# Query projections written from PSUM as 128x256 pieces, and queries stacked through DRAM instead of directly

## Chip, cores and metric

The kernel runs on one core of a Trainium2 chip. The metric is device time in microseconds (us) of one execution; the kernel before took 758.66 us (median of three runs, 758.6 to 760.47 us).

## What is computed

One transformer block on `x` of 2048 tokens by 512 features, in float32:

```python
qkv = layernorm(x) @ wqkv                      # 32 heads of 16 for q, k and v
scores = q @ k.T * 16 ** -0.5                  # per head
mask = (i - j >= 0) & (i - j < 256)            # sliding window of 256 tokens
o = softmax(where(mask, scores, -1e9)) @ v
h = x + o @ wo
z = layernorm(h)
out = h + (sigmoid(z @ w_gate) * (z @ w_up)) @ w_down      # 1376 inner features
```

## The kernel before

The 2048 tokens are 16 tiles of 128 and eight batches `b` of 256. Matrix products are made from float16 numbers: each operand is split into a high and a low half, and `mm3` (L359-362) issues three matmuls for each product, high by high, high by low and low by high. Such a split is made by two operations on a PSUM tile: the high half is copied out by ScalarE or VectorE (`copy`, which records L315 for ScalarE and L317 for VectorE), then VectorE computes what is left as a `scalar_tensor_tensor`.

**Order of the work.** Every step of the kernel is a piece of a generator. `TABLE`, a list of names, says which piece takes its next step, and with `/a`, `/v` or `/g` on which engine (ScalarE, VectorE, GpSimd) where a step may run on several. `Order` (L232-288) does no planning on the chip: the rows on each engine stand in the order of the table, and each engine works through its own rows in order. All the transfers are issued by SyncE (SP), also in order. `RINGS` (L302) gives the number of buffers of each kind; `s`=3 and `mm`=2 are PSUM rings, `chunk`=3 is the ring of weight chunks and normalised rows.

**Start.** `wqkv`, `wo` and the tiles of x are loaded. The greatest absolute value of each weight matrix is found (`am`, partly by ScalarE at L327, partly by VectorE at L329), passed through PE (L340) and made into a scale (`fq`, L344-348 on VectorE), with which the weights are split (ScalarE L315 `W<-wq,sq`, VectorE L481). The tiles of x are normalised (VectorE L497-501, ScalarE L510), split, and transposed by PE (L534) into `xT` (copied out at L315 or L317).

**Queries and keys.** `do_qk(b, c, jj)` (L562-587) makes for a batch the half `jj` of the queries (c=0) or the keys (c=1): 24 matmuls of 128x256 into a PSUM tile of 128 x 2 x 256, then the split into a staging tile, `sq` for queries and `sk` for keys. A key tile is split as one piece of 128x512. A query tile is split in two pieces of 64x512, since the partitions 0-63 hold one head of a pair and 64-127 the other, and the two go to different blocks of `sq`; the other blocks of `sq` stay zero, written once at the start. 

**Stacks.** The score matmuls contract over 96 rows: a stack holds high, high and low halves of the queries (`SQ`) against high, low and high halves of the keys (`SK`), 32 rows each. `do_queries(b, p)` (L606-614) fills a quarter of `SQ` for a batch by three transfers from `sq`, 128 KB each: four quarters, so twelve transfers in each batch and 96 in all. The next batch but one may overwrite `sq` when the four quarters are copied. `do_keys(b)` (L589-604) first writes `sk` to DRAM (`mem<-sk`, two transfers) and then reads the stack back (`SK<-mem`, 384 KB, twice in each batch).

**Attention.** `do_s` (L636-661) computes scores 128 rows by 320 columns into the `s` ring, and VectorE takes each row's maximum with the mask (L647, `junk<-sp,mask`, followed by the read of its accumulator, `mq`): 512 such row maxima in all. `do_m` turns them into four further rows of the stacks, so that `do_st` (L681-725) gives transposed scores with the maximum taken off (contraction over 100 rows, L711-722). ScalarE takes the exponentials (L689, into `pa` and `pb`), GpSimd cuts the mask (L695, L700), and `do_pv` (L729-761) multiplies with the values. The value projection (`W1v`, three 128x512 matmuls at each step), the output projection and the second layer norm stand between these on all the engines, and so do the scaling and splitting of the weights of the second half (`W0u`, `W`, `Tg`), whose `chunk` loads run throughout.

**Second half.** Gate, up and down products follow (L1096 and around). The last attention steps and the first gate matmuls overlap at about 400 to 440 us.

The parts that the change and the prediction touch are `do_qk`, `do_queries`, `do_keys`, the table, and `stacked`, which arranges the columns of `wqkv` before the launch.

Of the kernel before, what the change touches and what calls it, by code (L numbers as in the profile page):

```python
# [35 lines left out]
P = 128  # L36
# [29 lines left out]
load_w0 load_x0 load_w3 load_x1 load_w1 load_w2 zeros0 load_x3 load_w4 load_x2 load_w14 load_w10 load_w9 load_w15 load_w11 ln0*2 prep0/a*2 ln1 prep0/a ln0/v  # L66
load_w8 load_w12 load_x4 load_w5 load_w13 load_w6 load_x6 load_w7 ln1 prep0/v ln0/a prep0 ln1/a ln0/g prep0*2 ln4 ln1/a ln0 ln1/g zeros1 fill0 fill1 ln0/v
warm2 prep1/a prep0/a prep0 prep0/a prep0 prep0/a ln1 warm1 prep0 prep0/a ln1/a ln4 prep0 ln2 prep2/a qk0 ln2 qk1 qk0 prep2/a qk0 warm3 qk0 ln3 prep2/a ln5
prep2/a ln3 ln3/a qk0 qk1 qk0*3 qk1 ln2/v prep2 qk0/a prep2 qk1*5 ln4/v ln2/v ln3/v ln5 ln2/g qk0 ln4/a qk1/a prep2 warm4 warm0 ln2 warm5 qk1 fill2 ln3/g
# [4 lines left out]
amax1/a amax2 qk2*6 v1 qk2/v v1 qk2 v1 keys0 qk7 keys0 qk7*2 v1 qk7 prep3/a prep3/v prep3/g prep3/v ln9 amax0/v fill2 ln6 fill0 fill2 fill0 qk7*2 v1/v qk7
qk6*2 qk7 amax3/a amax4 queries3 qk6 warm8 qk7/v qk6*3 qk7 prep3/v keys0 qk6*2 v3 qk6/v v3 qk6 v3 queries2 amax7 queries5 queries6 keys1 ln4 v3 ln4/v amax4/a
amax2/a ln5/a v3/a prep3/g ln5/g ln7 fill1 fill0 fill2 s0*3 s0.0 s0.1 s0.2 s0*2 v4 s0.3 s0.4 s0*2 s0.5 s0.6 queries4 queries5 keys1 queries7 keys0 amax8 amax6
s1 ln5 s1 s1.0 s2 s1.1 v4 prep3/a*2 ln6/a s2.0 ln10 s0 s1 v4 s1 v4 s0.7 s1.2 s1.3 s1*2 s1.4 s1 s1.5 s1 s1.6 ln6/a ln5/a ln6/g prep3/g ln10 v4/a ln7/a amax7/a
# [1662 lines left out]
```

## Time and profile before

| what | us |
|---|---|
| median of three runs | 758.66 |
| the profiled execution, its own time | 758.37 |
| its span on the core | 756.0 |
| PE busy with matmuls | 732.3 |
| VectorE busy | 622.5 |
| ScalarE busy | 447.5 |
| GpSimd busy | 336.3 |

The time of an execution is some 2.4 us longer than the span that the profiler shows on the core. PE is the engine of matmuls; its weight loads (PEld) run beside them. The profile's windows give the busy time of each engine in a stretch of the span, its groups give the mean time of a kind of instruction, and its chain follows the work that ended last backwards from the end.

### The profile page before, as it was taken

What the parts mean: (1) busy time and instruction counts of PE and PEld (TensorE: products, weight loads), DVE (VectorE), ACT (ScalarE), POOL (GpSimd) and SP (SyncE); (2) the same over time, 40 slices, a digit from 0 to 9 for tenths busy, and PEclk for the clock granted to TensorE, in tenths of its full rate; (3) what the DMA queues carried; (4) which work ended last, traced back from release to release, by engine and by line L of the source; (5) the groups of instructions that cost most, each with busy time, mean ns of one, the idle gap of its engine ahead of it and who ended that gap; (6) DMA issues with size and microseconds to landing.
All of it is one profiled execution on the core that took longest, in us unless ns stands there. A gap on an engine that the chain in (4) does not pass through costs nothing.

```text
span 756.0 us, 18726 instructions
## 1 busy us (share of the span) xinstructions
PE 732.3 (97%) x6930; PEld 486.6 (64%) x6930; DVE 622.5 (82%) x1863; ACT 447.5 (59%) x784; POOL 336.3 (44%) x431
## 2 busy tenths in 40 slices
PE   4999999999999999999999899999999999999997
PEld 3777777777787677787665544454544755757573
DVE  6979999989888878788888999976899779587562
ACT  6845988787787877687768976523332224231401
POOL 7563557534553556445656612342230315345611
PEclk9999999999999999999999999999999999999999
DMA  9894665745948645445536768541775745545533
GB/s 324 209 249 125 146 132 109 178 123 103 194 110 171 120 84 146 92 80 141 112 78 143 182 144 240 137 77 37 153 174 123 129 91 112 101 98 110 116 53 97
DMA packets 182394, 100.96 MB, mean 134 GB/s; under 512 B 153440, under 2 KB 159584, under 8 KB 182304
## 3 DMA queue, kind: packets, MB, share of 16 engines
q1 hardware_dynamic: 182304, 99.78, 58.5%
q8 instruction: 54, 0.88, 0.5%
q14 instruction: 36, 0.29, 0.1%
HBM read 37.36 MB, written 13.11 MB: 67 GB/s over the span
## 4 chain that ended last, share of the span: by engine, by line
PE 83%; DVE 6%; ACT 3%; issue 3%; DMA 3%; POOL 1%; SPq 0%; DVEq 0%; ACTq 0%; POOLq 0%
PE mmp L362 25%; PE pvp L748 10%; PE sp L1096 9%; PE sp L660 8%; PE stp L1096 6%; PE sp L362 5%; PE stp L722 3%; PE stp L712 3%; PE stp L362 2%; PE pvp L1096 2%; PE sp L1368 2%; PE stp L711 2%; PE stp L713 2%; PE stp L1368 1%; ACT pa L689 1%
## 5 line engine op out<-in xcount | busy, mean ns | idle before, releaser
L647 DVE CUSTOM_DVE_ANT_0 junk<-sp,mask 128x320 bf16<-128x320 f32 (+4 forms) x512 | 214.6, 465 | 28.9 <-PE sp L660 27.0
L689 ACT ACTIVATE pa<-stp,kappa 128x512 f32<-128x512 f32 (+1 forms) x256 | 156.9, 646 | 32.8 <-PE stp L713 28.6
L660 PE MATMUL sp<-SK,SQ 96*128 96x64 f16 (+3 forms) x960 | 127.6, 232 | 1.4 <-DVE mq L647 0.2
L1096 PEld LDWEIGHTS <-SQ 128*128 128x128 f16 x756 | 73.9, 98 | 71.7 <-issue 1.6
L362 PE MATMUL mmp<-xT,W 128*128 128x256 f16 x768 | 110.1, 272 | 1.4 <-ACT xT L315 1.4
L689 ACT ACTIVATE pb<-stp,kappa 128x512 f32<-128x512 f32 x128 | 84.3, 686 | 22.2 <-PE stp L722 21.3
L660 PEld LDWEIGHTS <-SQ 96*128 96x128 f16 x960 | 79.6, 97 | 26.4 <-issue 8.4
L695 POOL TENSOR_SCALAR_AFFINE_SELECT pa<-pa 128x1024 f32<-128x1024 f32 x56 | 62.3, 1114 | 36.5 <-ACT pa L689 36.4
L362 PEld LDWEIGHTS <-W 128*128 128x128 f16 x768 | 69.9, 97 | 10.8 <-issue 2.0
L700 POOL TENSOR_SCALAR_AFFINE_SELECT pb<-pb 128x512 f32<-128x512 f32 x64 | 43.3, 679 | 64.2 <-ACT pb L689 63.7
L748 PE MATMUL pvp<-pa,VT 128*17 128x128 f32 (+1 forms) x1408 | 62.5, 307 | 0.0
L712 PE MATMUL stp<-SQ,SK 100*128 100x256 f16 x224 | 60.1, 270 | 0.0
L713 PE MATMUL stp<-SQ,SK 100*128 100x128 f16 x256 | 55.2, 218 | 0.2
L700 POOL TENSOR_SCALAR_AFFINE_SELECT pa<-pa 128x512 f32<-128x512 f32 x64 | 41.4, 656 | 29.4 <-ACT pa L689 28.9
L711 PE MATMUL stp<-SQ,SK 100*128 100x128 f16 x224 | 49.3, 220 | 3.4 <-ACT pa L689 2.3
L748 PEld LDWEIGHTS pvp<-pa,VT 128*17 128x17 f32 x1408 | 37.8, 97 | 22.9 <-issue 2.7
L362 PE MATMUL mmp<-WO,oT 128*128 128x512 f16 x192 | 50.1, 378 | 0.0
L362 PE MATMUL mmp<-W1v,xT 128*128 128x512 f16 x192 | 50.1, 378 | 0.0
L722 PE MATMUL stp<-SQ,SK 100*128 100x256 f16 x256 | 47.9, 272 | 0.9 <-ACT pa L689 0.7
L362 PEld LDWEIGHTS <-sq 128*128 128x128 f16 x288 | 27.9, 98 | 27.0 <-issue 0.4
L362 PE MATMUL mmp<-WD,hT 128*128 128x512 f16 (+1 forms) x192 | 44.4, 379 | 0.0
L647 DVE DVE_READ_ACCUMULATOR2_ANT mq<- 128x1 f32 x512 | 42.4, 83 | 0.1
(378 smaller groups left out, 1470.3 us busy)
## 6 DMA issues: line engine op xcount, KB each, us to landing
SQ<-sq SPq DMA_DIRECT2D x96, 128.0 KB
SK<-mem SPq DMA_DIRECT2D x16, 384.0 KB
chunk<-in_wd_dram SPq DMA_DIRECT2D x20, 256.0 KB
mem<-sk SPq DMA_DIRECT2D x8, 512.0 KB
out_dram<-WO SPq DMA_DIRECT2D x16, 256.0 KB
X<-in_x_dram SPq DMA_DIRECT2D x7, 512.0 KB
chunk<-in_wu_dram SPq DMA_DIRECT2D x12, 256.0 KB
xs<-X SPq DMA_DIRECT2D x10, 256.0 KB
```

The costliest lines, as they stand in the source:

```text
L362: PE.matmul(ps, a_of(a, k), b_of(b, k), start=(k == 0 and i == 0), stop=(k == n - 1 and i == 2))
L647: V.tensor_tensor_reduce(out=junk[:, c0:], in0=ps[:, c0:], in1=mask[:, c0:], scale=1.0, scalar=-3.0e38, op0=ALU.add, op1=ALU.max, accum_ou ...
L660: PE.matmul(ps[:, col:col + k1 - k0], q, SK[0:96, (2 * a + hf) % 5, 4 * (p % 2) + j, k0:k1], start=True, stop=True)
L689: S.activation(dst, a, AF.Exp, scale=kappa)
L695: G.affine_select(out=f, in_=f, pattern=[[0, 8], [-1, 128]], compare_op=ALU.is_gt, fill=0.0, base=0, channel_multiplier=1)
L700: G.affine_select(out=p, in_=p, pattern=[[0, 4], [1, 128]], compare_op=ALU.is_ge, fill=0.0, base=0, channel_multiplier=-1)
L711: PE.matmul(a[:, 0:128], ks(k0, g, j), qs(b, g, j, 0, 128), start=True, stop=True)
L712: PE.matmul(a[:, 128:384], ks(k0 + 1, g, j), qs(b, g, j, 0, 256), start=True, stop=True)
L713: PE.matmul(a[:, 384:512], ks(k0 + 3, g, j), qs(b, g, j, 128, 256), start=True, stop=True)
L722: PE.matmul(a[:, u, :], ks(k0 + 2, g, j + u), qs(b, g, j + u, 0, 256), start=True, stop=True)
L748: PE.matmul(ps[32 * j:32 * j + 17, u, q0:q1], VT[:, kt % 6, 8 * j + g, :], w[:, j, c:c + q1 - q0], start=first, stop=last, skip_group_chec ...
L1096: PE.matmul(out, x7[p][0][:, kk, MATS[a], ha, :], mv, start=first and i == 0, stop=i == 5, skip_group_check=True)
```

## The change

The columns of the query weights are put in another order by `stacked`, so that one 128-row matmul group of a query tile holds one head of every pair and the next group the other. A query tile is then split in two pieces of 128 partitions by 256 columns, not in two of 64 by 512; the keys' columns stay as they were.

`do_queries` no longer goes directly from `sq` to `SQ`. It writes both halves of `sq` to a DRAM tile `memq` (two transfers of 512 KB for a batch, zero blocks included), after which `sq` counts as copied, and then reads the stacks from `memq` (six transfers of 256 KB). All eight batches: 16 writes and 48 reads in place of 96 transfers. A half of a stack is written over only when all four groups of the half are done, where it was a quarter with two groups.

The table is new from end to end. PE has the same matmuls in nearly the same order. One line of the table is shown.

```diff
-load_w0 load_x0 load_w3 load_x1 load_w1 load_w2 zeros0 load_x3 load_w4 load_x2 load_w14 load_w10 load_w9 load_w15 load_w11 ln0*2 prep0/a*2 ln1 prep0/a ln0/v
+load_x0 load_w2 load_x1 load_w0 load_w1 load_w3 load_x3 ln0 fill1 fill0 ln0 load_w4 load_x2 ln1 ln0/v prep0/v ln1 prep0/a*2 ln0/a prep0/v ln0/g ln1/a prep0
-    RINGS = dict(s=3, st=2, mm=2, pv=1, chunk=3, ln=4, xn=1, hl=1, hlw=2, pp=3, rh=2, rt=2, os=2, whl=1, oT=1, mq=2, mt=2, mem=2,
+    RINGS = dict(s=3, st=2, mm=2, pv=1, chunk=3, ln=4, xn=1, hl=1, hlw=2, pp=3, rh=2, rt=2, os=2, whl=1, oT=1, mq=2, mt=2, mem=2, memq=2,
...
-    sq0 = keep.tile([P, 2, 4, 4, 2, 64], F16, name="sq0")
+    sq0 = keep.tile([P, 2, 2, 2, 4, 2, 64], F16, name="sq0")
...
-        times = 2 - c
-        e, = yield alt("qk", ACT_, ACT=0.49 * times + 0.22 * (times - 1), DVE=0.598 * times + 0.2 * (times - 1)), [e]
+        e, = yield alt("qk", ACT_, ACT=0.49 if c else 0.77, DVE=0.598 if c else 0.85), [e]
...
-            parts = [(ps[64 * u:64 * u + 64].rearrange("r j (i t) -> r j i t", t=64),
-                      [dst[64 * u:64 * u + 64, h, 2 * jj:2 * jj + 2, :, u, :] for h in range(2)]) for u in range(2)]
+            parts = [(ps[:, u].rearrange("p (i t) -> p i t", t=64), [dst[:, h, u, jj, :, u, :] for h in range(2)]) for u in range(2)]
...
-    def do_queries(b, p):
-
-        needs = [("qk", b, 0, j) for j in range(2)] + [(w, b - 2, 2 * p + u) for w in ("st", "s") for u in range(2) if b > 1]
-        for c in range(3):
-            e, = yield {DMA_: 0.58}, needs, [], 0.75
-            nc.sync.dma_start(SQ[b % 2][32 * c:32 * c + 32, 4 * p:4 * p + 4].rearrange("r j i u t -> r j (i u t)"),
-                              stage[int(b == 1)][0][p:P:4, c // 2].rearrange("r j i u t -> r j (i u t)"))
-        plan.mark(("queries", b, p), e)
-        plan.join(("copied", b), 4, e, lambda t: plan.mark(("copied", b, 0), t))
+    def do_queries(b):
+
+        x = stage[int(b == 1)][0]
+        m = None
+        for h in range(2):
+            e, *r = yield {DMA_: 0.5}, [("qk", b, 0, j) for j in range(2)], [] if h else ["memq"], 1.8
+            if not h:
+                n, m = r[0], dram.tile([2, 32, 16, 512], F16, name="memq", bufs=RINGS["memq"])
+            nc.sync.dma_start(m[h].rearrange("(u e) (q j) x -> (e q) u (j x)", u=2, j=2), x[:, h].rearrange("p u j i v t -> p u (j i v t)"))
+        plan.mark(("copied", b, 0), e)
+        w = e
+        for hf in range(2):
+            for c in range(3):
+                e, = yield {DMA_: 0.5}, [w] + [(k, b - 2, g) for k in ("st", "s") for g in range(4 * hf, 4 * hf + 4) if b > 1], [], 1.3
+                nc.sync.dma_start(SQ[b % 2][32 * c:32 * c + 32, 8 * hf:8 * hf + 8].rearrange("r s i u t -> r s (i u t)"), m[c // 2, :, 8 * hf:8 * hf + 8])
+            for p in range(2 * hf, 2 * hf + 2):
+                plan.mark(("queries", b, p), e)
+        plan.free("memq", n, e)
...
-        for p in range(4):
-            plan.add(do_queries(b, p))
+        plan.add(do_queries(b))
...
-    qk = w[:, :2 * D].reshape(D, 8, 4, 2, 16).transpose(0, 1, 3, 4, 2).reshape(D, 2 * D)
-    return np.ascontiguousarray(np.concatenate([qk, w[:, 2 * D:]], axis=1))
+    q = w[:, :D].reshape(D, 4, 4, 2, 16).transpose(0, 2, 1, 3, 4).reshape(D, 8, 2, 2, 16).transpose(0, 2, 3, 4, 1).reshape(D, D)
+    k = w[:, D:2 * D].reshape(D, 4, 4, 2, 16).transpose(0, 1, 3, 4, 2).reshape(D, D)
+    return np.ascontiguousarray(np.concatenate([q, k, w[:, 2 * D:]], axis=1))
```

Three places show what the new table moves. Lines of the code after stand two lower up to about L560 and five higher after L600, so L327 and L315 of before are L325 and L313 after.

The first is the start of ScalarE's rows, up to the copy of the first transposed x (`xT<-mmp`); `W,am<-wq` and `W,am<-wk` are the searches for the greatest weight, `W<-wq,sq` the high halves of the query weights, `RT` and `chunk` rows of the layer norm. Before:

```order
L327 ACTIVATE W_87,am<-wq 128x512 x3
L315 ACTIVATE RT<-chunk_70 128x512
L510 ACTIVATE chunk_71<-X,nb,rs 128x512
L315 ACTIVATE RT<-chunk_71 128x512
L327 ACTIVATE W_87,am<-wk 128x512
L315 ACTIVATE W_87<-wq,sq 128x512 x4
L315 ACTIVATE xT<-mmp 128x8x128
```

After:

```order
L325 ACTIVATE W_87,am<-wq 128x512 x2
L313 ACTIVATE RT<-chunk_70 128x512
L508 ACTIVATE chunk_71<-X,nb,rs 128x512
L313 ACTIVATE RT<-chunk_71 128x512
L313 ACTIVATE W_87<-wq,sq 128x512 x3
L313 ACTIVATE xT<-mmp 128x8x128
L313 ACTIVATE W_87<-wq,sq 128x512
```

One search in `wq` went to VectorE, the search in `wk` and the fourth `W<-wq,sq` stand behind the copy of `xT`. On VectorE the statistics of a third tile of x (L497-501) now stand ahead of the scale `fq`, where they stood behind it.

The second is SP between the first queries and the first keys' stack; `SQ_77`, `sq_88`, `sk_108` and `mem` are batch 0's, `SQ_85`, `sq_109` batch 1's, `chunk` the weights of the second half. Before:

```order
L611 DMA SQ_85<-sq_109 32x2048
L611 DMA SQ_77<-sq_88 32x2048 x2
L611 DMA SQ_85<-sq_109 32x2048
L826 DMA chunk_72<-in_wg_dram 128x512
L826 DMA chunk_70<-in_wg_dram 128x512
L611 DMA SQ_85<-sq_109 32x2048 x5
L826 DMA chunk_71<-in_wg_dram 128x512
L595 DMA mem<-sk_108 128x2x1024
L597 DMA mem<-sk_108 128x1024
L826 DMA chunk_72<-in_wg_dram 128x512
L611 DMA SQ_77<-sq_88 32x2048
L602 DMA SK<-mem 96x2048
```

After:

```order
L616 DMA SQ_77<-memq 32x4096 x3
L610 DMA memq<-sq_109 128x2x1024 x2
L831 DMA chunk_71<-in_wg_dram 128x512
L616 DMA SQ_77<-memq 32x4096
L831 DMA chunk_72<-in_wg_dram 128x512
L616 DMA SQ_77<-memq 32x4096
L616 DMA SQ_85<-memq 32x4096 x2
L591 DMA mem<-sk_108 128x2x1024
L593 DMA mem<-sk_108 128x1024
L831 DMA chunk_70<-in_wg_dram 128x512
L616 DMA SQ_85<-memq 32x4096
L598 DMA SK<-mem 96x2048
```

Up to and with this first `SK<-mem` SP issues 18 transfers `SQ<-sq` of 128 KB and five chunks of 256 KB before; after, four `memq<-sq` of 512 KB, eight `SQ<-memq` of 256 KB and three chunks. All the other transfers up to there (x, `wqkv`, `wo`, `mem`) are the same in number and size, though two more of the loads of x (512 KB each) now stand ahead of the first queries' transfer.

The third is ScalarE among the last exponentials (L689 of before, L694 after); `W0u`, `W`, `Tg` and `X` belong to the weights and the input of the second half. Before:

```order
L689 ACTIVATE pa<-stp,kappa 128x512 x3
L315 ACTIVATE X<-X 128x512
L315 ACTIVATE W0u<-chunk_70,su 128x512
L689 ACTIVATE pa<-stp,kappa 128x512
L689 ACTIVATE pb<-stp,kappa 128x512
L315 ACTIVATE W_87<-X,sg 128x2x256
L315 ACTIVATE W0u<-chunk_71,su 128x512
```

After:

```order
L313 ACTIVATE W0u<-chunk_70,su 128x512
L694 ACTIVATE pa<-stp,kappa 128x512 x2
L313 ACTIVATE W_87<-X,sg 128x2x256 x2
L694 ACTIVATE pb<-stp,kappa 128x512
L313 ACTIVATE W_87<-X,sg 128x2x256
L694 ACTIVATE pb<-stp,kappa 128x512
L313 ACTIVATE W0u<-chunk_71,su 128x512
L694 ACTIVATE pa<-stp,kappa 128x512
L313 ACTIVATE rh<-pvp_96 128x2x256
L694 ACTIVATE pa<-stp,kappa 128x512 x3
L313 ACTIVATE W0u<-chunk_72,su 128x512
L694 ACTIVATE pb<-stp,kappa 128x512
```

A third `W0u` now stands ahead of the last exponentials. On PE, 15 matmuls of the first gate product (`sp<-W,sq`, 128x512) stand between the last score matmuls in place of 12, and 45 of the first value projection's matmuls (`W1v`, 128x512) stand ahead of the first score matmul in place of 48.

More of the change, by code (lines that the diff above doesn't have):

```diff
@@ new lines @@
+mat1 mat3 down5*4 group5 down5 mix0 group5.5 group5 down5*2 mix0 mat6/a mat6/g pair2/v mat5/v group5.7 group5.4 group5.6 pair2 down5 pair3 mix0 group5.6
+group5.7 group5.5 group5.7 mat5/a group5.5*2 down5 group7 mat4/v group5.5/a mat5/v group5.6*2 group5.6/a group5.5/g group5.5 mix0.3/v group5.6/v mix0.1
+mix0.0/v group5.6 mix0.5 pair3*3 mix0.4/v mix0.1 pair3 group7 group7.0/a group7 mat4 group7 mix0*2 mat5 mat6 mix0*2 mix0.5 pair3 mix0.2 mix0.6 group7.2/a
+mix0*2 pair3/v pair3/a mix0.6 mix0.7 pair3/g mix0.8 pair3 group7.1 pair3 mix0*2 group6 mix0.10 mix0.9 group6*2 group6.0/a group6 group6.4*2 group6.1
@@ new lines @@
+group14 mat21 mat22 mat24 mix2.11 group14.6 group15.0/v group15 mat26/g group15.2/v group15.1 group14.4*2 group15 group14.7 mat26/v group15 group16 group14.7
+group15.3/v mat26/g group15.6 group15.5 group15.4*2 mix3 group16 group15 group14.5*2 mat27/v group14.7 group14.6 group16.0/v mat27/v group14.6 group16*2
+group14.6 group16.1 mat25/v group15.7 group16 mix3 mat27 mat23/a mat23/g group14.5 mix3.1 group14.6/a group14.5/a group14.5/g group14.6/v group15.5 mat23
+group15.6 mat25/v group16.2/v group16 group16.3/g group16.5 group16.4 group16.5 group16 mix3 group14.6 mat25 mat26 group14.5 mix3 group15.7 mix3.3/a
@@ new lines @@
+group16.4/a group16.6*2 mix3.0/a group16.6/a mix3*2 group16.4/g mix3.4/g mix2.12 mix3.5 mix3 group16.5/v group16.6/g group16.5/g mix3.6 mix3.1 mix3.7
+group16.4 mix3*2 group17 group16.7 mix3.6 mix3.2 group16.7 mix3.8 group16.7/v mix3*2 mix3.5 group16.7/g mix3.9 mix3.10 group17.0/v group17 down6 group17
+group17.1 group17*2 group16.7 down7 down6 group17.2/a group17.3/v group17 group17.5 group17 down6 down7 down6 group16.5 group16.6 down6 down7*3 down6*2 down7
+down6 down7 group17.7 group17.6 group17.7 group17.4 group17.6 group17.7 group17.4 group17.6*2 group17.6/a group17.6/g group17.6 mix3.12 down6*2 down7
@@ L230 @@
+group17.5*3 group17.5/v group17.5/g group17.5 down7 down6 mix3.11 down6 down7 down6 down7*3
 """
@@ L406, in tile_block @@
     for i, pool in enumerate((qk, wp)):
-        stage[i] = pool.tile([P, 2, 4, 4, 2, 64], F16, name=f"sq{i}") if i else sq0, pool.tile([P, 2, 4, B], F16, name=f"sk{i}")
+        stage[i] = pool.tile([P, 2, 2, 2, 4, 2, 64], F16, name=f"sq{i}") if i else sq0, pool.tile([P, 2, 4, B], F16, name=f"sk{i}")
     wsrc = {}
@@ L440, in zeros @@
     def zeros(i):
-        x = stage[i][0].rearrange("p h j i u t -> p (h j i u t)")
+        x = stage[i][0].rearrange("p h u j i v t -> p (h u j i v t)")
         e, = yield {POOL_: 1.75}, []
@@ L1563, in open_sq @@
         e, = yield {DVE_: 0.0}, [("copied", NB - 1, 0)]
[L1564 removed]
+        flat = sq0.rearrange("p h u j i v t -> p (h u j i v t)")
         X2.extend(flat[:, 1024 * i:1024 * i + 1024].rearrange("p (m q) -> p m q", m=2 * KT) for i in range(NP))
```

314 lines of the change are left out of this document (149 added, 165 removed).

## The prediction

> **What bounds the kernel now.** I read the page first: its span, its engines, and the sums of the chain that ended last.
>
> ```profile
> span 756.0 us, 18726 instructions
> PE 732.3 (97%) x6930; PEld 486.6 (64%) x6930; DVE 622.5 (82%) x1863; ACT 447.5 (59%) x784; POOL 336.3 (44%) x431
> PE 83%; DVE 6%; ACT 3%; issue 3%; DMA 3%; POOL 1%; SPq 0%; DVEq 0%; ACTq 0%; POOLq 0%
> ```
>
> PE is busy for 732.3 of 756.0 us and carries 83% of the chain. An average says nothing about the place, so I cut the span into stages by what PE does (start; queries and keys of the first batches; the first row maxima; the body of attention; the last exponentials; second half). Columns: PE, weight loads, VectorE, ScalarE, GpSimd, each with its count, then granted clock, DMA share, GB/s.
>
> ```profile
> 0.00:26.00 26.00, 13.52 (x144) 11.98 (x145) 18.54 (x51) 19.14 (x40) 20.07 (x36) 1.00 0.81 276
> 26.00:53.00 27.00, 27.00 (x216) 20.04 (x215) 22.50 (x49) 13.13 (x26) 14.45 (x17) 1.00 1.01 244
> 53.00:125.00 72.00, 70.16 (x803) 54.43 (x801) 69.42 (x339) 57.77 (x113) 39.72 (x56) 1.00 0.57 132
> 125.00:400.00 275.00, 274.85 (x3574) 205.35 (x3573) 232.53 (x886) 212.25 (x357) 142.88 (x185) 1.00 0.57 124
> 400.00:440.00 40.00, 35.79 (x421) 20.93 (x420) 37.67 (x80) 38.16 (x63) 22.68 (x27) 1.00 0.66 154
> 600.00:752.00 152.00, 151.81 (x960) 93.74 (x960) 103.63 (x190) 40.38 (x77) 57.24 (x62) 1.00 0.48 96
> ```
>
> So PE has no gap from 26 to 53, from 125 to 400 and from 600 on: there a faster copy is worth nothing. It waits in three places: at the start (12.48 us idle of 26), for VectorE at 53 to 125 (VectorE 69.42 of 72), and for ScalarE at 400 to 440 (38.16 of 40; PE idle 40.00 - 35.79 = 4.21 us). The chain in the second and the third place says the same; the first answer is for 99 to 103 us, the second for 400 to 440.
>
> ```profile
> by line: issue 73.1%; DVE mq L647 18.7%; DVE junk L647 14.7%
> by line: ACT pa L689 18.3%; PE pvp L748 13.6%; PE sp L362 13.2%; ACT pb L689 10.3%; PE mmp L362 8.1%; ACT W L315 8.1%; issue 6.6%; PE stp L722 4.0%; ACT W0u L315 2.9%; ACT Tg L315 2.9%; ACT X L315 2.8%; PE stp L711 2.8%; PE stp L712 2.5%; A
> ```
>
> At 99 to 103 us the row maxima (L647) pass PE's scores one by one through three buffers; at the end of attention the exponentials (L689) do. What the change is worth must come out in these three places.
>
> **The pieces.** A query piece costs now, and its nearest rows of 128x256 from PSUM are:
>
> ```profile
> L586 DVE SCALAR_TENSOR_TENSOR sq<-mmp,sq 64x512 f16<-64x512 f32 x32 | 22.0, 687 | 1.7 <-ACT sq L315 1.3
> L1398 DVE SCALAR_TENSOR_TENSOR WO<-sp,cd,WO 128x256 f32<-128x256 f32 x6 | 2.9, 480 | 4.5 <-PE sp L1381 3.6 <-PE sp L1368 0.9
> L315 ACT ACTIVATE sq<-mmp 64x512 f16<-64x512 f32 x32 | 18.8, 588 | 4.1 <-PE mmp L362 3.9
> L315 ACT ACTIVATE chunk<-stp 128x256 f32<-128x256 f32 x4 | 1.4, 376 | 5.3 <-PE stp L1368 5.3
> ```
>
> The counts stay (32 and 32). VectorE's piece falls from 687 to about 480 ns, 207 ns each, 6.6 us over 32; ScalarE's from 588 to about 376, 212 ns each, 6.8 us. Most of this lies where PE is full. In the row maxima's stage the pieces are these (VectorE, then ScalarE):
>
> ```profile
> 53.00:125.00 72.00, 0.00 (x0) 0.00 (x0) 4.12 (x6) 3.54 (x6) 0.00 (x0) 1.00 0.57 132
> ```
>
> Six pieces by 207 ns is 1.24 us at most. But the new table also moves work ahead of the same row maxima: by the order, up to the 112th of them VectorE gets two casts `hl` and one copy `sk` more and one `xn` less, which is two steps of 128x512 net, 2 x 0.69 = 1.37 us if each took as long as the 687 ns row. The ends are -0.13 and 1.24 us; shorter casts lie nearer the middle, and part of VectorE's work falls where it waits for PE anyway, so I take **0.2 us**. [...]
>
> **The start.** The rows up to the first query matmul:
>
> ```profile
> 9.00 0.16 DVE L473 TENSOR_REDUCE am<-am 128x1 f32<-128x4 f32 x1 [0.24 <-ACT W L327]
> 10.11 0.29 DVE L344 TENSOR_REDUCE fq<-sp 128x1 f32<-128x128 f32 x1 [0.95 <-PE sp L340]
> 10.76 0.61 ACT L327 ACTIVATE W<-wk 128x512 f16<-128x512 f32 x1
> 10.88 0.68 DVE L497 BATCH_NORM_STATS2 st<-X 128x6 f32<-128x512 f32 x1
> 11.28 0.19 ACT L327 ACTIVATION_READ_ACCUMULATOR W<-wk 128x1 f32 x1
> 11.37 2.54 ACT L315 ACTIVATE W<-wq,sq 128x512 f16<-128x512 f32 x4
> 12.48 2.73 DVE L481 SCALAR_TENSOR_TENSOR W<-wq,sq,W 128x512 f16<-128x512 f32 x4
> 13.82 1.00 ACT L315 ACTIVATE xT<-mmp 128x1024 f16<-128x1024 f16 x1
> 14.88 0.49 PE L362 MATMUL mmp<-xT,W 128*128 128x256 f16 x3 [1.40 <-ACT xT L315]
> ```
>
> The chain is ScalarE's: search in `wk`, four `W<-wq`, copy of `xT`, first matmul. After, a search (0.61 with a read of 0.19) and one `W` (2.54 / 4 = 0.63) no longer stand ahead of that copy: at most 0.8 + 0.63 = 1.4 us. Against it, the third tile's statistics, 0.68 and about 0.3 of small steps, now stand ahead of `fq`; 0.95 of that fits into VectorE's idle wait for PE. And the other operand comes next: VectorE's low halves of `W`, of which the first can't start before `fq` and the first `W`. So I take **0.63 us**; ends -0.3 (the statistics wait for their x) and 1.4.
>
> **Up to the first scores.** Three `W1v` matmuls move behind the first score matmul. Pieces of the chain (start, length):
>
> ```profile
> 25.99 5.24 PE mmp L362 x48
> 187.84 1.30 PE mmp L362 x6
> ```
>
> 48 matmuls of 256 columns take 5.24 us, and six of 512 columns 1.30, that is 0.217 each: three are **0.65 us**. PE is full here, so this and the start's 0.63 pass on in full, 1.28 us, if the stacks are there. That is the question, since the queries now pass through DRAM. On SP and PE:
>
> ```profile
> 48.57 0.33 SPq L602 DMA_DIRECT2D SK<-mem  x1
> 53.31 0.40 PEld L660 LDWEIGHTS <-SQ 96*128 96x128 f16 x4
> 53.52 0.33 PE L660 MATMUL sp<-SK,SQ 96*128 96x64 f16 x3
> 90.18 5.28 DMA SK<-mem
> ```
>
> The first `SK<-mem` is issued at 48.57 and has landed by 53.31, 4.74 us later; another of the kind, on the chain at 90.18, took 5.28. There is little slack. Ahead of it lie, after, four `memq` writes of 512 KB (2.10 MB more), 0.26 MB less of `SQ`, and two chunks less (0.52 MB): 1.31 MB more in all. In DMA's moving average at 41 to 49 us (40 equal slices) one sees what they cost:
>
> ```profile
> DMA  9999899898979999699999999999999989979993
> GB/s 215 164 195 225 164 205 184 143 205 143 246 123 195 154 215 195 113 205 266 184 205 225 236 307 369 410 410 410 410 410 348 318 328 328 328 276 430 348 338 51
> ```
>
> The first half, which is `SQ<-sq` into 32 partitions above all, runs at about 190 GB/s, the second, `mem<-sk` out of 128 partitions, at 330 to 410. `memq` has the form of the second: 2.10 MB at 380 is 5.5 us. Less `SQ` saves 0.26 / 0.19 = 1.4 us and the two chunks 0.52 / 0.26 = 2.0. Net 2.1 us. The two loads of x that now go ahead of the queries (1.05 MB) use part of the 19% of the first 26 us in which DMA is idle, which takes away about 1.4, and all of it starts with queries that are ready 0.6 earlier. So the stack comes about as early as PE can use it, or some tenths late: I take **1.0** of the 1.28 us. The later batches' queries need no such care: by the order, with the durations of these groups, at least 20 us of PE work lie between a batch's query matmuls and its first scores (an estimate), and a hop through DRAM takes the 5.28 us of the row above, twice.
>
> **The end of attention.** In 400 to 440 us ScalarE sets the pace and PE idles.
>
> ```profile
> 425.42 0.55 ACT W0u L315
> 433.94 2.59 PE sp L362 x12
> ```
>
> Twelve `sp<-W,sq` matmuls after the last scores take 2.59 us, 0.216 each. After, three more of them stand among the scores, where PE waits, so **0.65 us** less is left behind. ScalarE's own rows there are the same in number: one `W0u` (0.55) more ahead of the last exponentials, one `whl` less. Ends: -0.55, if that `W0u` is not paid for, and 0.65; the nearest row is the unchanged count, so 0.65.
>
> **The second half** has no PE gaps worth naming from 600 us, and the same matmuls: 0.
>
> **The sum** is made against the profiled execution, 758.37 us (span 756.0 and 2.4 around it), 0.3 below the median of the runs, 758.66: 758.37 - 1.0 - 0.2 - 0.65 = **756.5**. A measurement of this kernel can tell 0.3%, 2.3 us, from no change, so "same" is 756.4 to 760.9, and my forecast lies at its edge. Its own range runs from all the upper ends (1.4 + 0.65 + 1.24 + 0.65 = 3.94 us: 754.4) to the start and `W1v` at their lower end alone (0.35 us: 758.0).
>
> **Rivals.** *Nothing shows.* The terms are each lost in the next wait (the start in the stack, the end in ScalarE): 758.4, within some tenths. For it: PE is full in four of six windows. Against: each of the terms lies where PE waits.
>
> *All of it shows.* The start gives 1.4, `W1v` 0.65, the row maxima 1.24, the end 0.65 and, since ScalarE carries less there, half of its stage's idle 4.21: 6.0 us, 752.3. For it: these are the stages in which VectorE and ScalarE are the bound; against: the order shows other work in their place. [...]
>
> *Slower: the keys' stack comes late.* At 26 to 53 us DMA's share is 1.01 at 244 GB/s. If the additional 1.31 MB moves at that mean, and none of it in the early idle time, `SK<-mem` lands 5.4 us later, less 0.6 for the earlier start and 0.5 of slack: the first scores come 4.3 us late, PE has nothing to put in their place, and the time is 758.37 + 4.3 - 0.85 = 761.8. It decides from the point at which the stack lands after 53.2 us. For it: one queue in order, in which `memq` of batch 1 stands ahead of the keys of batch 0. Against: the rate of 330 to 410 for transfers of that form.
>
> **How the numbers follow.** Forecast 0.50, nothing shows 0.17, all shows 0.17, late stack 0.16. Half of the forecast's chance lies below 756.4: faster 0.25 + 0.17 = 0.42; same 0.25 + 0.17 = 0.42; slower 0.16. The range goes from 752.3 to 760.5, where seven tenths of the late stack's price would be paid.
>
> **What would show it.** In the profile after: pieces `sq<-mmp` of 128x256 near 480 and 376 ns; the first query matmul at 14.2 us; the first score matmul at 52.5 with PE idle ahead of it no more than 0.3 us; PE idle at 400 to 440 about 0.6 us less; no change in PE's idle time from 125 to 400. A first score matmul after 53.5 us, with PE waiting for `SK` or `SQ`, would prove me wrong towards slower; VectorE well under 69 of 72 us in the row maxima's stage, with the last row maxima earlier by more than 1.5 us, towards faster.

## The result and the profile after

The change takes 754.74 us (median of four runs, 753.75 to 755.04) against 758.63 us before (758.58 to 760.47). The ratio is 0.9941 with a 95% interval of 0.9923 to 0.9958, so the whole interval lies beyond the 0.3% that the forecast took as what can be told from no change. Run again beside the experiments, it gave 0.9947 (0.9934 to 0.996). The forecast was 756.5, within 752.3 to 760.5.

The profiled execution took 754.92 us with a span of 753.1, against 758.37 and 756.0. So 2.9 us of the gain of 3.45 lie in the span. What an execution takes outside it fell from 2.4 us to 1.8: it is 2.28 to 2.39 us in every run of the kernel before beside the experiments, and 1.72 to 2.01 in every run of a kernel whose queries go through DRAM, in the old order too. Why is open. The page of the change, first lines and the chain by engine:

```profile
span 753.1 us, 18635 instructions
PE 731.8 (97%) x6930; PEld 487.0 (65%) x6930; DVE 611.5 (81%) x1871; ACT 434.9 (58%) x776; POOL 341.6 (45%) x430
PE 80%; DVE 8%; DMA 4%; ACT 4%; issue 2%; SPq 1%; POOL 0%; DVEq 0%; ACTq 0%
```

PE's work is the same (731.8 for 732.3 us). VectorE lost 11.0 us and ScalarE 12.6 us of busy time, and of all that 2.9 us of span came out: most of it lies beside a full PE. The stages, with the columns of before:

```profile
0.00:26.00 26.00, 15.36 (x151) 13.56 (x152) 19.94 (x53) 18.15 (x36) 17.10 (x33) 1.00 0.96 339
53.00:125.00 72.00, 69.58 (x813) 55.09 (x812) 69.68 (x344) 55.72 (x115) 38.25 (x57) 1.00 0.65 147
125.00:400.00 275.00, 274.56 (x3566) 204.87 (x3565) 227.21 (x892) 208.21 (x362) 141.63 (x181) 1.00 0.63 144
400.00:440.00 40.00, 37.12 (x422) 21.28 (x420) 37.77 (x73) 37.66 (x62) 19.51 (x23) 1.00 0.62 149
```

In the first 26 us PE works 1.84 us more than before and DMA's share rises from 0.81 to 0.96, with two more of the loads of x early. At 400 to 440 us PE idles 2.88 us and not 4.21. The row maxima's stage (53 to 125) has kept its form, VectorE busy for 69.68 of 72 us where it was 69.42.

Where the span went, by the starts of five of PE's instructions in the trace (the last two are the start of the last matmul with the values, and the end of PE's work):

| us | before | after | after, again |
|---|---|---|---|
| first query matmul, batch 0 | 14.88 | 14.46 | 14.37 |
| first query matmul, batch 1 | 25.83 | 23.92 | 23.46 |
| first score matmul | 53.52 | 51.65 | 51.52 |
| last matmul with the values | 438.88 | 436.71 | 436.74 |
| end of PE's work | 752.26 | 749.33 | 749.23 |

1.9 to 2.0 us are won by the first scores, nearly all of it by the first queries of batch 1; 0.1 to 0.3 us from there to the end of attention; and 0.8 to 0.9 us in the second half.

The times of the start have a scatter that isn't the change's. PE's first matmuls begin 0.107 us apart for 128 columns and 0.213 for 256; from some moment on it is 0.056 and 0.109, so that they ran at half speed until then, though the granted clock of that window says 1.00. Full speed is there by 12.9 us in the profile before, by 15.3 and 12.4 in the two after, and by 18.0 in a run below that is the same kernel up to 400 us. Batch 0's 48 query matmuls, in the change and in that run:

```profile
14.46 5.78 PE L360 MATMUL mmp<-xT,W 128*128 128x256 f16 x48 [0.59 <-ACT xT L313]
14.04 7.31 PE L360 MATMUL mmp<-xT,W 128*128 128x256 f16 x48 [0.93 <-ACT xT L313]
```

In that run the first score matmul starts at 52.77 us, only 0.75 earlier than before. A measure without this scatter is the stretch from the start of batch 0's last query matmul to that of batch 1's first: 5.10 us before, 3.95 or 3.96 in all seven profiles that have the change's pieces and order there. The groups of the pieces after, and the six in the row maxima's stage:

```profile
L582 DVE SCALAR_TENSOR_TENSOR sq<-mmp,sq 128x256 f16<-128x256 f32 x32 | 11.9, 414 | 1.8 <-ACT sq L313 1.8
L313 ACT ACTIVATE sq<-mmp 128x256 f16<-128x256 f32 x24 | 7.9, 380 | 6.6 <-PE mmp L360 6.6
L317 DVE TENSOR_SCALAR sq<-mmp 128x256 f16<-128x256 f32 x8 | 3.0, 413 | 0.0
53.00:125.00 72.00, 0.00 (x0) 0.00 (x0) 2.19 (x6) 1.97 (x6) 0.00 (x0) 1.00 0.65 147
```

A low half takes 414 ns and not 687, a high half 380 and not 588 on ScalarE; the six pieces take 2.19 us of VectorE where they took 4.12.

The largest step, at batch 0's queries, can be seen in two timelines. Before (VectorE's low halves, then PE's transposes, which need the PSUM buffer that these free):

```profile
20.44 1.39 DVE L586 SCALAR_TENSOR_TENSOR sq<-mmp,sq 64x512 f16<-64x512 f32 x2 [0.49 <-ACT sq L315]
22.64 1.39 DVE L586 SCALAR_TENSOR_TENSOR sq<-mmp,sq 64x512 f16<-64x512 f32 x2
24.08 0.62 PE L534 MATMUL mmp<-identh,RT 128*128 128x128 f16 x8 [1.13 <-DVE sq L586]
25.83 0.38 PE L362 MATMUL mmp<-xT,W 128*128 128x256 f16 x2
```

After:

```profile
19.84 0.74 DVE L582 SCALAR_TENSOR_TENSOR sq<-mmp,sq 128x256 f16<-128x256 f32 x2
20.97 0.76 DVE L582 SCALAR_TENSOR_TENSOR sq<-mmp,sq 128x256 f16<-128x256 f32 x2 [0.38 <-ACT sq L313]
22.73 0.40 PE L532 MATMUL mmp<-identh,RT 128*128 128x128 f16 x4 [0.48 <-POOL RT L320]
23.92 2.25 PE L360 MATMUL mmp<-xT,W 128*128 128x256 f16 x19
```

Before, PE stood for 1.13 us until the second pair was done; after, this wait is gone, and the pair ends at 21.73 and not at 24.03. It isn't the shorter piece alone: the second pair also starts 1.67 us earlier, since ScalarE's high halves ahead of it are shorter (0.66 for 1.20 us) and the new order has put the scale of the value weights (`fv`) behind it on VectorE.

### The profile page after: what moved, and what is told of

It reads as the page before. It is cut to its first block, busy times and chain, and to the rows that moved or that the text cites. A ratio compares the mean times of both kernels' runs of the same rounds, so it can differ in the third digit from the quotient of the medians.

```text
span 753.1 us, 18635 instructions
## 1 busy us (share of the span) xinstructions
PE 731.8 (97%) x6930; PEld 487.0 (65%) x6930; DVE 611.5 (81%) x1871; ACT 434.9 (58%) x776; POOL 341.6 (45%) x430
## 4 chain that ended last, share of the span: by engine, by line
PE 80%; DVE 8%; DMA 4%; ACT 4%; issue 2%; SPq 1%; POOL 0%; DVEq 0%; ACTq 0%
PE mmp L360 26%; PE pvp L753 10%; PE sp L665 8%; PE sp L1101 8%; PE stp L1101 5%; PE stp L727 3%; PE stp L717 3%; PE sp L360 3%; PE pvp L1101 2%; PE stp L716 2%; PE sp L1373 2%; PE stp L718 2%; PE stp L360 2%; ACT pa L694 1%; PE stp L1373 1%
## 5 line engine op out<-in xcount | busy, mean ns | idle before, releaser
L694 ACT ACTIVATE pa<-stp,kappa 128x512 f32<-128x512 f32 (+1 forms) x256 | 156.8, 647 | 38.1 <-PE stp L718 34.2
L665 PE MATMUL sp<-SK,SQ 96*128 96x256 f16 (+3 forms) x960 | 128.5, 232 | 1.4 <-DVE mq L652 0.8
L694 ACT ACTIVATE pb<-stp,kappa 128x512 f32<-128x512 f32 x128 | 85.3, 686 | 27.0 <-PE stp L727 25.3
L705 POOL TENSOR_SCALAR_AFFINE_SELECT pb<-pb 128x512 f32<-128x512 f32 x64 | 41.1, 646 | 47.1 <-ACT pb L694 44.4
L320 POOL TENSOR_TENSOR X<-X 128x352 f16<-128x352 f32 (+1 forms) x18 | 19.3, 1078 | 55.3 <-ACT X L313 33.5
```

The lines of the kernel that those rows point to most:

```text
L665: PE.matmul(ps[:, col:col + k1 - k0], q, SK[0:96, (2 * a + hf) % 5, 4 * (p % 2) + j, k0:k1], start=True, stop=True)
L694: S.activation(dst, a, AF.Exp, scale=kappa)
L705: G.affine_select(out=p, in_=p, pattern=[[0, 4], [1, 128]], compare_op=ALU.is_ge, fill=0.0, base=0, channel_multiplier=-1)
```

## Experiments

Each ratio is to the kernel before, run beside on the same chip, where its median was 759.09 to 759.91 us.

**Old pieces in the new order.**

```diff
-            parts = [(ps[:, u].rearrange("p (i t) -> p i t", t=64), [dst[:, h, u, jj, :, u, :] for h in range(2)]) for u in range(2)]
+            parts = [(ps[64 * u:64 * u + 64].rearrange("r j (i t) -> r j i t", t=64),
+                      [dst[64 * u:64 * u + 64, h, 2 * jj:2 * jj + 2, :, u, :] for h in range(2)]) for u in range(2)]
...
-            nc.sync.dma_start(m[h].rearrange("(u e) (q j) x -> (e q) u (j x)", u=2, j=2), x[:, h].rearrange("p u j i v t -> p u (j i v t)"))
+            nc.sync.dma_start(m[h].rearrange("r (p j) x -> (r p) (j x)", p=4), x[:, h].rearrange("p j i u t -> p (j i u t)"))
```

Expected: 

> The new table and the queries' way through DRAM, but the query weights' columns and the split pieces as before (64x512). Theory (pieces pay where PE waited for them: at the start, and a little among the row maxima; the table gives the rest): the first batch-1 query matmul 0.6 to 1.2 us later than in the change, the row maxima's stage up to 1 us longer, 756.0 to 757.0 us. Rival 'the pieces are all of it': 758.6, as before. Rival 'the table is all of it': 754.7, as after.

Measured: 760.12 us, ratio to before 1.0007 (0.9998 to 1.0017). All the gain is gone, and 5.1 us against the change run beside it (754.99), which is more than any of the three theories had. The first batch-1 query matmul is at 25.04 us, the first score at 52.77, both 1.12 behind the change. That looks like the expected step, but no query matmul ran at half speed in this profile: from batch 0's last to batch 1's first it takes 5.57 us and not 3.95, a step of 1.6. And it goes on: the 61st of the 960 score matmuls is 2.27 us late (74.37 to 76.64), the last 4.95 (398.68 to 403.63), in steps of 0.2 to 0.9 us between 118 and 326 us of the change's time. The second step stands at batch 2's pieces, among the row maxima:

```profile
62.81 1.19 ACT L313 ACTIVATE sq<-mmp 64x512 f16<-64x512 f32 x2 [1.50 <-PE mmp L360]
64.05 1.39 DVE L583 SCALAR_TENSOR_TENSOR sq<-mmp,sq 64x512 f16<-64x512 f32 x2
65.88 0.43 PE L666 MATMUL sp<-SK,SQ 96*128 96x64 f16 x2 [0.22 <-DVE mq L653]
66.68 1.19 ACT L313 ACTIVATE sq<-mmp 64x512 f16<-64x512 f32 x2 [1.92 <-PE mmp L360]
68.07 1.39 DVE L583 SCALAR_TENSOR_TENSOR sq<-mmp,sq 64x512 f16<-64x512 f32 x2
69.84 0.24 PE L666 MATMUL sp<-SK,SQ 96*128 96x192 f16 x1 [0.26 <-DVE mq L653]
```

The same place in the change, in which no wait of PE stands behind a pair:

```profile
61.70 0.66 ACT L313 ACTIVATE sq<-mmp 128x256 f16<-128x256 f32 x2 [1.50 <-PE mmp L360]
62.91 0.75 DVE L582 SCALAR_TENSOR_TENSOR sq<-mmp,sq 128x256 f16<-128x256 f32 x2
65.01 0.66 ACT L313 ACTIVATE sq<-mmp 128x256 f16<-128x256 f32 x2 [2.04 <-PE mmp L360]
66.23 0.75 DVE L582 SCALAR_TENSOR_TENSOR sq<-mmp,sq 128x256 f16<-128x256 f32 x2
```

VectorE does a pair in one stretch, in which it takes no row maximum, and the score buffers run full: a pair of 1.39 us outlasts them, one of 0.75 doesn't. The two waits shown are 0.48 of the 1.15 us that are lost up to the 61st score matmul; the rest stands in no wait that the profile lists.

**New pieces in the old order.** The table of before, with the new steps of the queries in the old places:

```diff
-queries0*2 load_x5 queries1 queries3 queries1 queries3 load_x8 load_x7 queries2 queries0
+queries0*2 load_x5 queries0*3 load_x8 load_x7 queries0*3
```

Expected: 

> The new pieces (128x256) and the way through DRAM, each step at its old place in the old table (the two writes where the batch's first quarter stood, a half's three reads where the later of its two quarters stood). Theory: the wait for the second pair of low halves at 22.7 to 24.1 us shrinks by about 0.65 us, the row maxima gain some tenths, the moved W1v and first-gate matmuls stay behind: 757.0 to 757.8 if the stacks come in time. Rival 'late stack': the writes add 2.1 MB ahead of the first keys' stack and nothing is taken away ahead of it, so the first scores come 2 to 4 us late: 759.5 to 761.5. Rival 'pieces are all of it': 754.7.

Measured: 773.41 us, ratio 1.0184 (1.0169 to 1.0199). The rival's mechanism came about, at far more than its price: the first score matmul starts at 60.57 us, 7.05 later than before, where it had 2 to 4, and the time is 13.6 us longer, where it had 1 to 3. The chain up to the first score matmul, and PE's row:

```profile
33.08 9.99 DMA memq<-sq
...
43.09 4.44 DMA SQ<-memq
...
47.60 8.48 DMA mem<-sk
...
56.15 4.38 DMA SK<-mem
```

```profile
60.57 0.48 PE L662 MATMUL sp<-SK,SQ 96*128 96x64 f16 x3 [7.39 <-DMA SK<-mem]
```

The writes of batch 1's queries take 9.99 us in the full queue (DMA's share is 1.02 from 26 to 53 us). Their six reads, due tens of microseconds later, go out at 43.1 us, when the writes have landed; the keys of batch 0 come behind them and take 8.48 us to DRAM, and the stack is read back from 56.15. PE stands for 7.39 us. It goes on through attention, where SP stands at such reads again and again; first the waits of SP for `memq` here, then in the change:

```profile
SPq L613 <- DMA memq<-sq: 19.0, 12, 3.8
```

```profile
SPq L616 <- DMA memq<-sq: 3.9, 3, 3.4
```

Twelve waits and 19.0 us, three and 3.9: the new order puts other rows between a write and its reads.

**Only the way through DRAM.** Old order, old pieces; the diff is that of both runs above together.

Expected: 

> The old table and the old pieces (64x512), only the way of the queries goes through DRAM. Theory (the hop is covered after the start, and at the start it competes with the keys' stack): the first SK<-mem is issued later than at 48.6 us; the time is 758.6 to 760 if the slack before the first scores takes it, with the first scores no earlier than 53.5 us. Rival 'late stack': first scores at 55.5 to 57.5 us and 760.6 to 762.6. Rival 'fewer transfers help' (12 to 8 for each batch on SP): under 758.

Measured: 775.45 us, ratio 1.0198 (1.0175 to 1.0221); the first score matmul at 62.51 us. The five runs lie in two groups, at 771.57 and 772.0 and at 775.45 to 776.24. So by itself the way through DRAM costs some 13 to 17 us in this order, by the ratio's interval. Whether the new pieces take some of it back (773.41 with them) can't be told, since the two intervals overlap.

**The old order with SP's rows put right at one place.** Two loads of x ahead of batch 0's queries, batch 1's queries behind both stacks of batch 0's keys:

```diff
-queries0*2 load_x5 queries0*3 load_x8 load_x7 queries0*3
+load_x5 load_x8 queries0*5 load_x7 queries0*3
...
-keys1 keys0 amax8 amax6
+keys1 keys0 queries1*8 amax8 amax6
```

Expected: 

> The old order with new pieces and the way through DRAM, as in the second run, but on SP two loads of x stand ahead of batch 0's queries and all the transfers of batch 1's queries behind batch 0's second SK<-mem. Theory (the late first scores are the price of what stands ahead of the keys' stack on SP, not of the way through DRAM): first scores at 52.5 to 54.0 us in place of 60.6, the time 5 to 7 us less than there, 766 to 768.5. Rival 'DMA is simply full': first scores later than 57 us.

Measured: 770.37 us, ratio 1.0137 (1.0116 to 1.0158). SP's row for the stack:

```profile
46.21 0.32 SPq L594 DMA_DIRECT2D SK<-mem  x1
```

`SK<-mem` is issued at 46.21 us and not at 56.15, and the first score matmul starts at 52.78, as the theory had it: the stack was late by what stood ahead of it on SP, not since DMA was full. The total fell by 3.0 us only (3.6 by the ratios), short of the 5 to 7 expected, since the next thing in the queue became late. ScalarE's wait and the chain from 53 to 70 us:

```profile
ACT chunk L321 <- DMA chunk<-in_wg_dram: 13.7, 2, 7.7
by line: DMA chunk<-in_wg_dram 50.3%; POOL hl L316 13.7%; issue 10.5%; POOL SQ L425 6.7%; POOL SK L425 5.6%; SPq L827 5.1%; ACT chunk L321 4.2%; POOL rs L497 3.0%; POOL nb L499 1.6%; ACT xn L504 0.1%
```

SP stood still between the writes to `memq` (52.46) and the reads (57.53), with the weight chunks behind; ScalarE waited for a chunk with its other rows behind that, and PE stood for 3.7 us up to 72.3, for a query piece that came late in this way:

```profile
72.27 1.46 PE L356 MATMUL mmp<-xT,W 128*128 128x256 f16 x6 [3.66 <-DVE sq L578]
```

**One step of the value projection ahead of the first scores, less and more.** Less, and more:

```diff
-... ln9 v3 s0*3 v3
+... ln9 s0*3 v3*2
```

```diff
-... ln9 v3 s0*3 v3
+... ln9 v3*2 s0*3
```

Expected (less): 

> The change with one step of the first value projection (three W1v matmuls) taken from ahead of the first score matmul to behind it: 42 stand ahead in place of 45. Theory (what is moved behind the first scores lies in the stage that waits for VectorE, and costs nothing there): the first scores 0.65 us earlier than in the change, at 51.0 us, the time 0.3 to 0.65 us less, 754.1 to 754.5 on a chip where the change takes 754.75. Rival 'the keys' stack is the bound now': first scores stay at 51.6 with PE waiting for SK. Rival 'taken back later': first scores earlier, but no gain by the last scores.

Expected (more): 

> The change with three W1v matmuls put back ahead of the first score matmul, 48 as before. Theory: first scores 0.65 us later, at 52.3 us, and 0.3 to 0.65 us more at the end. Rival 'taken back later' (the stage of the row maxima has enough waits to take them anyway): the first scores later, the end the same.

Measured: 754.8 us, 0.9935 (0.9919 to 0.9951), and 754.96 us, 0.9937 (0.992 to 0.9954). Neither can be told from the change. In their profiles the step is there: the last key matmuls stand at 46.58 and 46.64 us, alike, and the first scores at 50.62 and 51.98. With less, the lead is taken back by the 61st score matmul: relative to the key matmuls it is then where it is in the change. With more, the 61st score matmul is 0.63 us later than in the change by the same measure. So up to there the step fills waits behind the first scores once, in the change, and a second one finds none left. By the last score matmul it can't be told any more: that starts 352.34 us behind the key matmuls with more, 352.42 with less, and 351.72 and 351.86 in the two profiles of the change.

**One step of the first gate product put back.**

```diff
-st63.4 early0 st63 split0/a early2 early0 st63 st63.6
+st63.4 early0 st63 split0/a early2 st63 early0 st63.6
```

Expected: 

> The change with one step of the first gate product (three matmuls of 512 columns) put back behind the last scores: 12 stand ahead of them, as before, and not 15. Theory: PE idles 0.65 us more at 400 to 435 us and the end comes 0.4 to 0.65 us later. Rival 'ScalarE sets the end alone': the last scores come as early as with the step ahead of them, and the step costs its 0.65 us in full behind; rival 'free': no difference, since another wait follows.

Measured: 755.03 us, 0.9934 (0.9917 to 0.9951): no difference. In the traces 21 matmuls of the first gate product stand ahead of the last pair of transposed score matmuls in the change, 15 before and 18 here (ahead of the last pair but one 15, 12 and 15): the new order moved two steps ahead of the last pair, and this run puts one of them back. The last transposed score matmul comes 0.64 us earlier than with the step ahead of it, and the last one with the values at the same distance from there back (38.04 us behind the last of the row maxima's scores, in the change 38.03 and 38.04). PE's busy time at 400 to 440 us is what it is in the change:

```profile
400.00:440.00 40.00, 37.12 (x429) 21.68 (x428) 37.72 (x79) 38.14 (x63) 20.57 (x25) 1.00 0.62 154
```

So these three matmuls filled no wait: PE is busy for all of 430 to 440 us in the change, and the step takes its time at either place. The outcome is that of the rival 'free', though not for its reason. What won 0.82 us in this stage (38.86 to 38.04) is something else in the order, which wasn't isolated. It is the order's, not the pieces': the stretch is 38.85 or 38.86 us in all four profiles with the old table, new pieces among them, and 38.03 to 38.06 in all ten with the new one, old pieces among them.

**ScalarE's start.**

```diff
-prep0 prep0/a ln1/a load_x8 load_w6 load_w15 load_w14 load_x6 load_x4 prep0 prep0/a zeros1
+prep0 prep0/a load_x8 load_w6 load_w15 load_w14 load_x6 load_x4 prep0 prep0/a ln1/a zeros1
```

Expected: 

> The change with ScalarE's start put back in one point: the copy of xT behind the fourth W<-wq, not ahead of it. Theory (ScalarE's chain sets the first query matmul): the first query matmul 0.5 to 0.7 us later, at 15.0 to 15.2 us, first scores later by as much. Rival 'VectorE's low halves of W set it': first query matmul at 14.5 to 14.7 us and no difference behind.

Measured: 755.52 us, 0.9940 (0.9919 to 0.9961): no difference in the time that can be told. The first query matmul is at 14.38 us, not at 15.0 to 15.2, but in this execution the scale of the query weights was ready early. From the start of the scale's last step (`sq<-fq` on VectorE) to the first query matmul it takes 3.71 us here, and 3.09 or 3.10 in all nine profiles with the change's order there. So the place of the copy is worth 0.62 us, as the theory of ScalarE's chain had it, and the rival fails. That the first query matmul of batch 1 comes late, at 25.17 us, isn't this: batch 0's 48 took 7.11 us, the first of them at half speed, as in the kernel above (25.04), where kernels alike up to there have 23.46 to 23.92.

**Low halves twice**, in batch 0 alone, and in batches 2 to 7:

```diff
-        for x, (hi, lo) in parts:
+        for x, (hi, lo) in parts * (2 if c == 0 and b == 0 else 1):
```

```diff
-        for x, (hi, lo) in parts:
+        for x, (hi, lo) in parts * (2 if c == 0 and b > 1 else 1):
```

Expected (batch 0): 

> The change with the low halves of batch 0's query pieces computed twice (four operations of about 0.37 us more on VectorE, the same numbers written again); all the rest as in the change. Theory (PE waits at the start for the PSUM buffer that these free): first batch-1 query matmul 0.6 to 1.1 us later, and the end by as much. Rival 'pieces at the start are hidden': no more than 0.2 us.

Expected (batches 2 to 7): 

> The change with the low halves of the query pieces of batches 2 to 7 computed twice (24 operations of about 0.41 us more, 9.9 us of VectorE's time). By the old pieces' run, where the loss behind the first scores was 3.9 us with about 0.27 us more on VectorE and 0.2 on ScalarE for each piece, theory 'the new order leaves no slack around the pieces' expects 3 to 5 us more at the end, in steps at each batch. Rival 'the body is PE's' (my forecast: only the six pieces among the first row maxima count): at most 1.5 us more, all before 125 us.

Measured, batch 0: 755.24 us, 0.9939 (0.992 to 0.9957), no difference in time. In the profile the wait is back where it was before the change:

```profile
20.89 0.62 PE L532 MATMUL mmp<-identh,RT 128*128 128x128 f16 x8 [0.78 <-DVE sq L582]
22.30 0.61 PE L532 MATMUL mmp<-identh,RT 128*128 128x128 f16 x8 [0.34 <-DVE sq L582]
```

PE waits 0.78 + 0.34 us for VectorE's pieces, and from the last of batch 0's query matmuls to the first of batch 1's it takes 4.99 us and not 3.95. This profile's start happened to be 0.8 us early, so the end doesn't show it. Mechanism shown, price in the time not.

Batches 2 to 7: 756.14 us, 0.9949 (0.9931 to 0.9967), not to be told from the change either. In the profile 0.95 us are lost between the first and the 61st score matmul, at batch 2's pieces, and nothing from there to the end of attention. The load was smaller than expected: VectorE's busy time rises by 4.7 us (616.2 for 611.5) and not by 9.9, and four such operations behind one another take 1.41 us where the pair takes 0.75. That is as long as the old pair of 1.39, and it costs most of what the old pieces lose in that stretch, so the low halves' time is the cause there. The theory's 3 to 5 us failed, the rival held.

**Both halves twice, in all batches.**

```diff
-        for x, (hi, _) in parts:
+        for x, (hi, _) in parts * (2 - c):
...
-        for x, (hi, lo) in parts:
+        for x, (hi, lo) in parts * (2 - c):
```

Expected: 

> The change with both halves of every query piece computed twice (the same numbers written again), so that a pair of pieces holds ScalarE for about 1.5 us in place of 0.76 and VectorE for 1.65 in place of 0.83; the old pieces held them for 1.18 and 1.37. Layout and transfers stay those of the change. Theory (the run with old pieces lost its 5 us by the time of the pieces, high and low together): at least as much as there, 759.5 to 764, with steps at the start, at 60 to 70 us and in the body of attention at the batches' query pieces. Rival 'it was the transfers out of the old layout': no more than the 1 to 2 us of the run with the low halves twice, 756 to 757.

Measured: 758.08 us, ratio 0.9984 (0.9974 to 0.9994): about 3 us more than the change, between the theory and the rival. At batch 2 the four pieces hold ScalarE for 1.21 us and VectorE for 1.41, not for the 1.5 and 1.65 expected: as long as the old pair (1.19 and 1.39). The windows at 125 to 400 us, of this kernel, and of the one with old pieces:

```profile
125.00:400.00 275.00, 273.99 (x3557) 204.28 (x3556) 233.71 (x911) 210.72 (x371) 141.25 (x181) 1.00 0.62 143
```

```profile
125.00:400.00 275.00, 273.43 (x3550) 203.72 (x3548) 233.42 (x885) 210.41 (x360) 140.16 (x179) 1.00 0.61 141
```

With as much load on VectorE and ScalarE (233.7 and 210.7 us, 233.4 and 210.4) PE idles 1.01 and 1.57 us here, in the change 0.44. The time of the pieces explains some three fifths of what the old pieces cost, by the ratios; the last 2 us may be the form of the transfers out of the old staging tile or the order of the halves within a pair, and stay open.

## Why the prediction was right, and where not

**The bound** was read rightly: from 125 to 400 us PE idles 0.15 us before and 0.44 after, while VectorE lost 5.32 and ScalarE 4.04 us there.

**The pieces** were sized by rows that were a little too dear for VectorE (480 for 414 ns, so 207 for a relief of 273) and right for ScalarE (376 for 380). The counts were not as read: eight of the 32 high halves now run on VectorE. In the window of the row maxima the six low halves gave 1.93 us, above the 1.24 that I took as the most.

**The start** had the failed step. I took 1.0 us for the time up to the first scores; it was 1.9 to 2.0 in the two profiles of the change, and 0.75 in the one whose matmuls ran longest at half speed. ScalarE's chain was read rightly: from the scale's last step to the first query matmul it takes 3.09 us where it took 4.07, while the statistics ahead of the scale make it 0.55 us later (11.36 for 10.81). That leaves 0.42 of the 0.63 forecast. The three `W1v` matmuls are 0.65 us less of PE's work there. What I left out is a wait that was in the trace: 1.13 us of PE for the low halves of batch 0 at 24.08. I had costed the pieces in the row maxima's stage only, with the sentence that most of the rest lies where PE is full; but the window 0 to 26 us said that PE idles there 12.48 us, and batch 0's four pieces lie in it. The cut of 0.28 us for a late stack was needless: `SK<-mem` is issued 3.3 us earlier than before, and PE doesn't wait for it.

```profile
45.28 0.32 SPq L598 DMA_DIRECT2D SK<-mem  x1
51.65 0.33 PE L665 MATMUL sp<-SK,SQ 96*128 96x64 f16 x3
```

**The row maxima and the last exponentials**, 0.2 and 0.65 us in the sum, gave 0.1 to 0.3 together. In the new order the pieces' time is worth about 1 us up to the 61st score matmul (0.95 to 1.15, by the runs with longer pieces). That the sum shows less I put down to other work that the order moved there, as forecast; no run isolates it. At the end PE's wait did fall, by 1.33 us in the window, but the three gate matmuls that were put back filled none of it, so that the mechanism of this term was wrong for them; that the stage gave 0.82 us where I had 0.65 is luck. Of the other three that moved there no run tells. And the gain there is mostly given back between the first and the last score matmul, which take 0.54 us more than before.

**The second half** was put at 0 and gave 0.8 to 0.9 us. Its order is new as well, and I hadn't compared it. From the last matmul with the values to the end of PE's work it takes 311.9 to 312.9 us in the ten profiles of the new order and 313.4 to 314.9 in the four of the old, so the gain goes with the order, while its size is uncertain by 1 us.

**Outside the span** the sum kept 2.4 us as they were. They are 1.8 now, some 0.55 us of the gain, with the cause open.

**The slower rival** was not what the change does, but it is real: with the old order on SP the stack was 7 us late, by the mechanism named (transfers of batch 1's queries ahead of batch 0's keys). My estimate of 4.3 us was low, since it went by bytes and left out that SP stands still at the read until the write has landed (there the reads went out at 43.09 and 56.15 us, behind writes of 9.99 and 8.48 us).

So the direction and the range were right, and the forecast's 2.2 us below the median of before were 3.9. The first query matmul and `W1v`, whose mechanisms held in the profiles, make 1.07 us of that, though the run with `W1v` put back shows nothing of it in the time. The wait that was left out, the second half and the time outside the span, which were put at nothing, are the larger part.

## What to carry to other kernels

A written-out order and the pieces it places are one thing: here the old pieces in the new order gave back all the gain, and the new path and pieces in the old order cost 13.6 us. Before an early step of two profiles is compared, see at what speed the matmuls ahead of it ran (here full speed came at 12.4 to 18.0 us). When costing a shorter piece, list every wait that ends with it, at the start too, before calling the rest hidden. With the hop through DRAM SP, which issues in order, stood at the reads until the writes had landed (twelve waits and 19.0 us in the old order, three and 3.9 in the change), so look at what stands behind such a read and who waits for it.

## What the runs showed of the hardware

A long wait of PE cost more than its length here. In the run with the old order PE stood from 53 to 60.5 us, and then (PE busy first, the granted clock third from the end):

```profile
53.00:60.50 7.50, 0.18 (x1) 0.00 (x0) 0.26 (x1) 3.77 (x9) 1.77 (x3) 0.65 0.64 205
60.50:62.00 1.50, 1.38 (x7) 0.67 (x7) 1.18 (x9) 0.51 (x1) 1.44 (x3) 0.50 1.10 411
62.00:64.00 2.00, 2.00 (x16) 1.53 (x15) 0.81 (x8) 0.00 (x0) 1.44 (x2) 0.50 1.03 309
64.00:66.00 2.00, 2.00 (x10) 0.85 (x9) 1.67 (x8) 1.54 (x2) 1.14 (x2) 0.63 0.46 142
66.00:70.00 4.00, 3.73 (x33) 2.65 (x32) 3.62 (x25) 1.91 (x4) 1.89 (x4) 1.00 0.00 0
```

The granted clock is 0.50 for the first 3.5 us of work and whole again by 66 us: some 2.5 us of full-clock time on top of the 7.4 waited. If it steps once within each window, between 1.00 and 0.50, the means of 0.65 and 0.63 put its fall at about 55.2 us, 2.1 us after PE's last matmul ended, and its return at 65.5, 4.9 us after the first matmul behind the wait (an estimate). In the change no wait of PE behind its start is longer than 0.9 us, and the clock is 1.00 in every window shown. At the start that column can't be relied on: it says 1.00 where the matmuls of 256 columns begin 0.213 us apart and where they begin 0.109 apart.

A split piece of 64 partitions by 512 columns cost VectorE 687 ns, as much as one of 128 by 512, as the keys' and the queries' groups of before show:

```profile
L586 DVE SCALAR_TENSOR_TENSOR sq<-mmp,sq 64x512 f16<-64x512 f32 x32 | 22.0, 687 | 1.7 <-ACT sq L315 1.3
L586 DVE SCALAR_TENSOR_TENSOR sk<-mmp,sk 128x512 f16<-128x512 f32 x16 | 11.0, 687 | 1.5 <-ACT sk L315 1.3
```

Here the time went with the columns: as many numbers, laid across all the partitions in 256 columns, take 414 ns, 0.6 of it.
